# Hash attention and an MLP on one core: when squares, loads and block transposes of the next batch are issued

## Chip, cores and metric

One core of a Trainium2 chip runs the whole program in one launch. The metric is the device time of an execution in microseconds (us); lower is better.

## What is computed

The reference takes q, k and v of 4 batches, 8 heads, 768 tokens and 64 columns, and a projection of 64 by 6. Each query and key gets a bucket number from the signs of its 6 projections; a query attends only to keys of its own bucket. The attention output, rearranged to 768 rows of 512 per batch, goes through a normalisation and a two-layer MLP with a residual:

```
q_bits = (q @ proj > 0);  q_bucket = sum(q_bits * 2**arange(6))      # k likewise
scores = where(q_bucket == k_bucket, q @ k.T / 8, -1e9)
attn   = softmax(scores);  x = (attn @ v) as (4, 768, 512)
xn     = (x - mean(x)) / sqrt(var(x) + 1e-6) * g_ln
out    = x + relu(xn @ w_ch1) @ w_ch2                                  # 512 -> 2048 -> 512
```

## The kernel before

**Chunks.** The work is cut into 12 chunks, three of 256 queries for each batch, numbered 0 to 11; chunk n belongs to batch n // 3. A chunk's attention (`att_units`, L397) is 12 groups: for each, four score matmuls (L417), one exponential on ScalarE (L423) and eight value matmuls (L451). The scores of a group are emitted before the values of the group ahead of it. The MLP of a chunk (`mlp_steps`, L484) runs one chunk later: `norm` on VectorE (L523), a DMA transpose of the normalised rows into `xnT` (L541, on SP's queue), eight `up` steps (L568) that read `xnT`, and eight `down` steps (L590), the latter still one chunk later.

**The stage "chunk n"** (n = 3 to 11) therefore holds on TensorE: the 12 groups of chunk n, first the `down` steps of chunk n - 2 and then the `up` steps of chunk n - 1. `interleave` (L652) emits them: after the scores of the next group come the "lone" operations of this group (`lone[u]`, L676), then fillers up to a share of the chunk. `norm` is the first filler. The string of `plan` (L778) for chunk n has three parts: the first two are mixed with the two halves of the `down` steps, the last with the `up` steps.

**Preparing a batch** (class `Prep`, L184) takes, for each half of four heads:
- `L`, `load_half` (L136): q and k from memory into `qnat` and `knat`, natural layout. For batches 2 and 3 these are two DMAs of 384 KB for each of q and k, on SP's queue. Each of the two tile names has four buffers, so a load of batch b waits until the same half of batch b - 2 is done with.
- `W`, `load_values` (L159): one DMA of 768 KB into `vnat`, which has one buffer; `V` (L340) casts it on GpSimd and adds sums.
- `N`, `narrow` (L242): a cast on GpSimd to `nat16`; `T`, `operands` (L269): a DMA transpose of `nat16` into `slots` (L272), and behind it a DMA that copies the odd tokens within `slots` (L279).
- `B`, `blocks` (L250): four 32x32 block transposes on VectorE; `H`, `hashes` (L281): 32 hash matmuls, two VectorE operations, a DMA of the bits to a buffer in memory (L301, `bits_d`), and four DMAs that bring the bit rows back into `slots` (L303); these wait until `bits_d` has landed.
- `Q`, `squares` (L198): four ScalarE activations for each half that square q and k in place and accumulate the sums, for a check at the end. They are the last reader of `qnat` and `knat`.
- `E`, `share` (L353): one matmul and a copy.

**What sets the order.** Chunks 0, 1 and half of 2 are written out by hand (`first_two`, L696, table `also`). From there on the scheduler of the language may move instructions on each engine and queue, save those that are marked `tc.keep_in_program_order`. Before, the squares, the block transposes and the DMA transposes of batches 2 and 3 are marked, the loads are not. Each engine and SP's queue run their instructions strictly in order: a DMA that has to wait holds every DMA behind it on SP.

`alone` (L794) and `spread` (L798) put the block transposes and squares at groups: `B`s at the first four groups of the chunk, `Q`s evenly over the rest.

Of the kernel before, what the change touches and what calls it, by code (L numbers as in the profile page):

```python
# [28 lines left out]
def kernel(  # L29
# [11 lines left out]
    nc = tc.nc  # L41
# [94 lines left out]
    def load_half(b, half):  # L136

        h0 = half * H // 2
        t = {}
        for nm in "qk":  # L140
            t[nm] = nat.tile([P, H // 2, NC, D], F32, tag=f"{nm}nat", name=f"{nm}nat")

        if b == 0 and half == 0:
            nc.scalar.dma_start(out=proj1[0:D, 0, 0:n_bits], in_=proj)
        cuts = [[0, 1, 2, 4] if half == 0 else [0, 2, 4], [0, 4], [0, 2, 4], [0, 2, 4]][b]
        for lo, hi in zip(cuts, cuts[1:]):
            for nm, src in (("q", q), ("k", k)):
                eng = nc.gpsimd if b == 1 else nc.scalar if nm == "k" and hi - lo == 1 else nc.sync
                eng.dma_start(
                    out=t[nm][:, lo:hi],  # L150
                    in_=src[b, h0 + lo : h0 + hi].rearrange("h (p c) d -> p h c d", p=P),
                )
        if b == 0 and half == 0:
            nc.scalar.activation(wake2[:, 0:1], wake2[:, 1:2], AF.Exp)
            t["v"] = load_values(b, half, 0, 2)
            load_values(b, half, 2, 4, t["v"])
        return t

    def load_values(b, half, lo=0, hi=None, t=None):  # L159
        hi = H // 2 if hi is None else hi  # L160
        h0 = half * H // 2
        eng = nc.gpsimd if (b, half) == (1, 0) else nc.sync
        if t is not None:
            pass
# [7 lines left out]
        eng.dma_start(  # L172
            out=t[:, lo:hi],
            in_=v[b, h0 + lo : h0 + hi].rearrange("h (p c) d -> p h c d", p=P),
        )
        return t

    def copy_by(eng, dst, src):
# [5 lines left out]
    class Prep:  # L184
# [13 lines left out]
        def squares(self, half, a, j):  # L198

            src = self.tiles[half]["qk"[a]][:, 2 * j : 2 * j + 2].rearrange("p h c d -> p (h c d)")  # L200
            col = (2 * self.b + half) * 2 + j
            tc.keep_in_program_order(
                nc.scalar.activation(src, src, AF.Square, accum_out=sq[:, a, col : col + 1])  # L203
            )

        def tokens(self, h, par):

# [61 lines left out]
        def operands(self, half):  # L269


            done = nc.sync.dma_start_transpose(  # L272
                out=self.pair_places(half)[:, :, 0, :],
                in_=self.nat16[half].rearrange("p h a c d -> p (h a c d)"),
            )
            if self.b > 1:
                tc.keep_in_program_order(done)
            dst = self.pair_places(half)
            nc.sync.dma_start(out=dst[0:D, :, 1, :], in_=dst[D:P, :, 0, :])  # L279

# [90 lines left out]
        def part(self, kind, half):  # L371

            if kind == "T":
                return [(0, lambda: self.operands(half))]
            if kind == "H":
                return [(1300, lambda: self.hashes(half))]
            if kind == "N":
# [318 lines left out]
    def first_two():  # L696
# [8 lines left out]
        def keep_awake(n, pool=ps_mm, tag="mm"):  # L705
# [50 lines left out]
            16: [lambda: nxt.operands(0)],  # L756
# [19 lines left out]
            units[n][u][1]()  # L776

    plan = {  # L778
# [6 lines left out]
    }  # L785

    def prepare(text):
# [10 lines left out]
    def spread(text, n):  # L798

        ops = [f for _, f in prepare(text)]  # L800
        first = len(ops) if n < 2 * NP else 4 * text.count("B")
        rest = n - first
        out = [[f] for f in ops[:first]] + [[] for _ in range(rest)]
        for i, f in enumerate(ops[first:]):
            out[first + i * rest // (len(ops) - first)].append(f)
        return out

    def mixed(a, b):

# [9 lines left out]
    for n in range(2, len(chunks)):  # L819
# [19 lines left out]
        interleave(units[n][FIRST if n == 2 else 0 :], fillers, after, begun=True, lone=spread(alone.get(n, ""), 3 * NP - (FIRST if n == 2 else 0)))  # L839
# [190 lines left out]
```

## Time and profile before

| What | Value |
|---|---|
| Median of 3 runs | 323.79 us (323.53 to 324.67) |
| The profiled execution, own time | 321.0 us |
| Its span, first to last instruction | 319.2 us |
| Granted TensorE clock, mean | 0.995 |
| TensorE matmuls busy | 304.4 us, 95% |
| ScalarE / VectorE / GpSimd busy | 215.9 / 182.6 / 79.8 us |
| Chain that ended last | TensorE 82%, VectorE 7%, DMA 5% |

Times in the traces below count from the start of the span, in us. A row of the timeline has the start, the duration, the engine (SPq is SP's queue of DMA issues, PE is TensorE), the line, the operation, "output<-input" and a count; brackets hold the time that the engine sat idle just before, and what ended that idle time. For a DMA the duration is that of the issue, not of the transfer. A row of the windows view has the stretch, its length, the busy time of each engine with a count, the granted clock, the busy share of the DMA engines and what they moved.

### The profile page before, as it was taken

What the parts mean: (1) busy time and instruction counts of PE and PEld (TensorE: products, weight loads), DVE (VectorE), ACT (ScalarE), POOL (GpSimd) and SP (SyncE); (2) the same over time, 40 slices, a digit from 0 to 9 for tenths busy, and PEclk for the clock granted to TensorE, in tenths of its full rate; (3) what the DMA queues carried; (4) which work ended last, traced back from release to release, by engine and by line L of the source; (5) the groups of instructions that cost most, each with busy time, mean ns of one, the idle gap of its engine ahead of it and who ended that gap; (6) DMA issues with size and microseconds to landing.
All of it is one profiled execution on the core that took longest, in us unless ns stands there. A gap on an engine that the chain in (4) does not pass through costs nothing.

```text
span 319.2 us, 7982 instructions
## 1 busy us (share of the span) xinstructions
PE 304.4 (95%) x3338; PEld 227.1 (71%) x3338; DVE 182.6 (57%) x410; ACT 215.9 (68%) x273; POOL 79.8 (25%) x101
## 2 busy tenths in 40 slices
PE   7899989999999989999999999999999999999992
PEld 6565677858768748769768778778679688686661
DVE  1779965854674775646774774543634634446321
ACT  3688785855658857977768868979767568673110
POOL 3745210096060281044171160200200200202000
PEclk9999999999999999999999999999999999999998
DMA  7999999359696397492583183030110410200201
GB/s 242 362 216 316 196 316 107 69 133 236 157 241 145 97 289 167 138 271 101 197 167 97 11 164 98 11 93 9 35 66 2 43 58 2 68 35 14 87 11 66
DMA packets 65035, 40.95 MB, mean 128 GB/s; under 512 B 47216, under 2 KB 60016, under 8 KB 64992
## 3 DMA queue, kind: packets, MB, share of 16 engines
q1 hardware_dynamic: 60528, 31.85, 41.4%
q0 software_dynamic: 4096, 8.13, 10.9%
q8 instruction: 28, 0.46, 0.6%
q10 hardware_dynamic: 368, 0.39, 0.4%
q14 instruction: 15, 0.12, 0.1%
HBM read 27.98 MB, written 6.88 MB: 109 GB/s over the span
## 4 chain that ended last, share of the span: by engine, by line
PE 82%; DVE 7%; DMA 5%; ACT 2%; issue 2%; ACTq 0%; DVEq 0%
PE hp L568 25%; PE o L590 24%; PE sc L417 17%; PE av L451 9%; DVE slots L182 4%; DMA xnT<-xn 4%; PE hash L288 3%; ACT ex L423 2%; DMA knat<-in_k_dram 1%; DVE bits L324 1%; PE tpose L223 1%; PE hash L319 1%; DVE x L476 1%; ACT qnat L203 1%; DVE qkT L233 0%
## 5 line engine op out<-in xcount | busy, mean ns | idle before, releaser
L423 ACT ACTIVATE ex<-sc,expb 128x1024 bf16<-128x1024 f32 x144 | 159.9, 1116 | 64.5 <-PE sc L417 64.2
L568 PE MATMUL hp<-xnT,w_sb 128*128 128x256 bf16 x768 | 97.9, 273 | 2.5 <-DMA xnT<-xn 2.1
L590 PE MATMUL o<-w_sb,hbuf 128*128 128x512 bf16 (+1 forms) x400 | 95.7, 370 | 0.0
L417 PE MATMUL sc<-slots 70*128 70x256 bf16 x576 | 87.8, 272 | 1.8 <-DVE slots L182 1.7
L568 PEld LDWEIGHTS <-w_sb 128*128 128x128 bf16 x768 | 72.7, 98 | 12.4 <-DMA xnT<-xn 2.7
L451 PEld LDWEIGHTS <-ex 128*128 128x128 bf16 x1152 | 53.7, 98 | 18.1 <-ACT ex L423 3.1
L417 PEld LDWEIGHTS <-slots 70*128 70x128 bf16 x576 | 50.6, 97 | 16.3 <-issue 2.7
L451 PE MATMUL av<-vaug,ex 128*128 128x65 bf16 x1152 | 59.3, 194 | 0.9 <-ACT ex L423 0.8
L129 DVE TENSOR_SCALAR hbuf<-hp 128x512 bf16<-128x512 f32 x47 | 32.5, 691 | 46.8 <-PE hp L568 45.9
L590 PEld LDWEIGHTS <-hbuf 128*128 128x128 bf16 x400 | 36.9, 97 | 27.1
L546 POOL TENSOR_SCALAR rs<-mv 128x2 f32<-128x2 f32 x11 | 7.0, 635 | 153.8 <-DVE mv L531 153.7
L133 ACT ACTIVATE hbuf<-hp 128x512 bf16<-128x512 f32 x49 | 29.2, 596 | 18.5 <-PE hp L568 18.4
L595 DVE SCALAR_TENSOR_TENSOR x<-o,rs,x 128x512 f32<-128x512 f32 (+1 forms) x25 | 18.0, 719 | 32.3 <-PE o L590 32.3
L476 DVE TENSOR_TENSOR x<-x,rc 128x256 f32<-128x256 f32 x36 | 19.2, 533 | 1.0
L468 DVE TENSOR_SCALAR rc<-av 128x4 f32<-128x4 f32 x36 | 5.7, 157 | 21.8 <-PE av L451 21.8
L248 POOL CAST nat<-qnat 128x1536 bf16<-128x1536 f32 x6 | 8.9, 1489 | 29.9 <-DMA qnat<-in_q_dram 27.7
L532 DVE SCALAR_TENSOR_TENSOR xn<-x,mv,gbc 128x512 bf16<-128x512 f32 x22 | 15.5, 741 | 0.1
L469 DVE TENSOR_TENSOR x<-av,vsum 128x256 f32<-128x256 f32 x36 | 14.9, 415 | 0.0
L530 DVE BATCH_NORM_STATS2 stats<-x 128x6 f32<-128x512 f32 x22 | 14.0, 675 | 0.1
L203 ACT ACTIVATE knat<-knat 128x768 f32<-128x768 f32 x16 | 13.5, 841 | 0.0
L203 ACT ACTIVATE qnat<-qnat 128x768 f32<-128x768 f32 x16 | 13.4, 838 | 0.0
L253 DVE STREAM_TRANSPOSE bt<-qnat 128x768 f32<-128x768 f32 x12 | 11.6, 970 | 2.7 <-DMA qnat<-in_q_dram 2.6
(88 smaller groups left out, 213.9 us busy)
## 6 DMA issues: line engine op xcount, KB each, us to landing
out_dram<-x SPq DMA_DIRECT2D x23, 256.0 KB
vnat<-in_v_dram SPq DMA_DIRECT2D x6, 768.0 KB
qnat<-in_q_dram SPq DMA_DIRECT2D x11, 384.0 KB
knat<-in_k_dram SPq DMA_DIRECT2D x11, 384.0 KB
w_sb<-in_moe_w_ch_dram POOLq DMA_DIRECT2D x4, 1024.0 KB, 16.0
slots<-slots SPq DMA_DIRECT2D x6, 384.0 KB
qnat<-in_q_dram POOLq DMA_DIRECT2D x2, 768.0 KB, 20.8
knat<-in_k_dram POOLq DMA_DIRECT2D x2, 768.0 KB, 22.1
```

Of the source, the lines that this page charges most:

```text
L129: nc.vector.tensor_scalar_max(dst, src, 0.0)
L133: nc.scalar.activation(dst, src, AF.Relu if relu else AF.Copy)
L203: nc.scalar.activation(src, src, AF.Square, accum_out=sq[:, a, col : col + 1])
L417: nc.tensor.matmul(sc[:, i, :], sl[0:K1, h, 1, kj * P : (kj + 1) * P], sl[0:K1, h, 0, q0 : q0 + CT],)
L423: nc.scalar.activation(ex, sc, AF.Exp, bias=expb[:, 1:2] if b else expb[:, 0:1], scale=scale if b else scale / Q_SCALE,)
L451: nc.tensor.matmul(av[:, h - ha, qi, :], state[g][:, i, qi * P : (qi + 1) * P], va[:, h, CMAP[b][kj], :], start=(b > 0 and (g, i, qi) == ( ...
L469: nc.vector.tensor_tensor(xv, num, vs[:, ha : ha + 2, :].unsqueeze(2).to_broadcast([P, 2, TT, D]), op=AOP.add,)
L476: nc.vector.tensor_tensor(xv, num, rc.unsqueeze(3).to_broadcast([P, 2, TT, D]), op=AOP.mult)
L532: nc.vector.scalar_tensor_tensor(xn[:, :, i, :], x[:, i, :].rearrange("p (o d) -> p o d", d=P), mv[:, i, 0:1], gbc.rearrange("p (o d) -> p ...
L568: nc.tensor.matmul(hp[:, i, :], w1_sb[:, dt, nt * P : (nt + 1) * P], st["xnT"][:, dt, :], start=(dt == 0), stop=(dt == ND - 1),)
L590: nc.tensor.matmul(o2, st["h"][:, nt, i * P : (i + 1) * P], w2_sb[:, nt, cols], start=(nt == 0), stop=(nt == NH - 1),)
L595: nc.vector.scalar_tensor_tensor(x[:, i, cols], o2, st["rs"][:, i : i + 1], x[:, i, cols], op0=AOP.mult, op1=AOP.add,)
```

## The change

- **Squares.** The squares of batch 0, half 0 move from chunk 2 to four groups at the end of `first_two`; those of every later half move one chunk ahead (batch 0, half 1 from chunk 3 to chunk 2, and so on; chunk 8 keeps four of its eight). No chunk has more than four.
- **Loads.** The loads of batches 2 and 3 (q, k and v) are marked to stay in program order on SP, and `plan` puts most of them into its middle part: behind the DMA transpose of the same chunk and ahead of the hashes.
- **Odd tokens.** The copy of odd tokens becomes a step of its own, `O`, with its own place in the plan.
- **Blocks of batch 2, half 0** move from groups 0 to 3 of chunk 3 to groups 2 to 5.

In the built program the DMAs of SP's queue stand in this order around chunks 2 to 5 (the names are those of the plan; "bits" is L301, "rows" the four of L303):

```
before  T11 W20 out O11 bits L20a rows L20b out xnT(3) | out T20 O20 L21(q q) out bits rows x2 L21(k k) rows x2 W21 xnT(4)
        | out T21 O21 L30(q q) out bits rows x2 L30(k k) rows x2 W30 xnT(5)
after   T11 L20(q) out L20(k q k) O11 bits out W20 rows x4 xnT(3) | out T20 O20 L21(q k q k) out bits rows x4 xnT(4)
        | out T21 O21 W21 L30(q k q k) out bits rows x4 xnT(5)
```

```
 def load_half(b, half):
...
-                eng.dma_start(
+                done = eng.dma_start(
...
+                if b > 1:
+                    tc.keep_in_program_order(done)
...
 def load_values(b, half, lo=0, hi=None, t=None):        # likewise
...
 def squares(self, half, a, j):
-            tc.keep_in_program_order(
-                nc.scalar.activation(src, src, AF.Square, accum_out=sq[:, a, col : col + 1])
-            )
+            done = nc.scalar.activation(src, src, AF.Square, accum_out=sq[:, a, col : col + 1])
+            if (self.b, half) > (0, 0):
+                tc.keep_in_program_order(done)
...
+        def odd_tokens(self, half):                    # was the end of operands
+
             dst = self.pair_places(half)
             nc.sync.dma_start(out=dst[0:D, :, 1, :], in_=dst[D:P, :, 0, :])
...
-            24: [ups[2]],
-            25: [ups[3], lambda: nxt.hashes(0)],
-            26: [ups[4], lambda: nxt.blocks(1, 0, 0)],
-            27: [ups[5], lambda: nxt.blocks(1, 0, 1)],
+            24: [ups[2], lambda: prep.squares(0, 0, 0)],
+            25: [ups[3], lambda: nxt.hashes(0), lambda: prep.squares(0, 0, 1)],
+            26: [ups[4], lambda: nxt.blocks(1, 0, 0), lambda: prep.squares(0, 1, 0)],
+            27: [ups[5], lambda: nxt.blocks(1, 0, 1), lambda: prep.squares(0, 1, 1)],
...
     plan = {
-        2: "V10 N11 W11 | T11 H11 L20 | E10 V11 W20",
-        3: "E11 N20 | T20 L21 | H20",
-        4: "V20 W21 L30 N21 | T21 | H21 E20",
-        5: "V21 W30 L31 | E21",
-        6: "V30 W31 N30 | T30 | H30 E30",
-        7: "V31 N31 | T31 | H31 E31",
+        2: "V10 N11 W11 | T11 L20 O11 H11 | E10 V11 W20",
+        3: "E11 N20 | T20 O20 L21 | H20",
+        4: "V20 N21 | T21 O21 W21 L30 | H21 E20",
+        5: "V21 | W30 L31 | E21",
+        6: "V30 N30 | T30 O30 W31 | H30 E30",
+        7: "V31 N31 | T31 O31 | H31 E31",
     }
...
     alone = {
-        2: "Q00", 3: "B20 Q01", 4: "B21 Q10", 5: "Q11", 6: "B30 Q20", 7: "B31 Q21", 8: "Q30 Q31",
+        2: "Q01 QQQQ..",
+        3: "B20 Q10 ..BBBBQ.Q.QQ",
+        4: "B21 Q11 BBBBQ.Q.Q.Q.",
+        5: "Q20 Q..Q..Q..Q..",
+        6: "B30 Q21 BBBBQ.Q.Q.Q.",
+        7: "B31 Q30 BBBBQ.Q.Q.Q.",
+        8: "Q31 Q..Q..Q..Q..",
     }
```

`spread` now reads these strings: one character for each group, a dot for none.

More of the change, by code (lines that the diff above doesn't have):

```diff
@@ L171, in load_values @@
             t = nat.tile([P, H // 2, NC, D], F32, tag="vnat", bufs=1, name="vnat")
-        eng.dma_start(
+        done = eng.dma_start(
             out=t[:, lo:hi],
@@ L175, in load_values @@
         )
+        if b > 1:
+            tc.keep_in_program_order(done)
         return t
@@ L201, in squares @@
             col = (2 * self.b + half) * 2 + j
-            tc.keep_in_program_order(
-                nc.scalar.activation(src, src, AF.Square, accum_out=sq[:, a, col : col + 1])
-            )
+            done = nc.scalar.activation(src, src, AF.Square, accum_out=sq[:, a, col : col + 1])
+            if (self.b, half) > (0, 0):
+                tc.keep_in_program_order(done)
         def tokens(self, h, par):
@@ L374, in part @@
                 return [(0, lambda: self.operands(half))]
+            if kind == "O":
+                return [(0, lambda: self.odd_tokens(half))]
             if kind == "H":
@@ L794, with spread @@
     alone = {
-        2: "Q00", 3: "B20 Q01", 4: "B21 Q10", 5: "Q11", 6: "B30 Q20", 7: "B31 Q21", 8: "Q30 Q31",
-    }
[L798 to L806, printed above, removed]
+        2: "Q01 QQQQ..",
[5 more added lines that the diff above has]
+        8: "Q31 Q..Q..Q..Q..",
+    }
+    def spread(text):
+        *ops, places = text.split()
+        todo = {op[0]: [f for _, f in prepare(op)] for op in ops}
+        return [[todo[c].pop(0)] if c != "." else [] for c in places]
     def mixed(a, b):
@@ L838 @@
             after = units[n + 1][0]
-        interleave(units[n][FIRST if n == 2 else 0 :], fillers, after, begun=True, lone=spread(alone.get(n, ""), 3 * NP - (FIRST if n == 2 else 0)))
+        interleave(units[n][FIRST if n == 2 else 0 :], fillers, after, begun=True, lone=spread(alone[n]) if n in alone else ())
     tc.no_sync_barrier()
```

2 lines of the change are left out of this document (1 added, 1 removed).

## The prediction

> **What bounds the kernel now.** I read the page's chain of work first, then the busy times by chunk, then the idle time of TensorE, and last SP's queue, because the idle time led there.
>
> ```profile
> PE 82%; DVE 7%; DMA 5%; ACT 2%; issue 2%; ACTq 0%; DVEq 0%
> ```
>
> TensorE sets the end; no other engine is worth shortening for itself. The windows view shows where TensorE's time is more than its work. The stretches run from the first `down` matmul of one chunk to that of the next: the end of the hand-written part, then chunks 3, 4, 6, 8 and 10. The last two rows are stretches in which the loads fill the DMA engines.
>
> ```profile
> 46.80:61.80 15.00, 14.72 (x196) 12.48 (x194) 9.35 (x17) 10.63 (x13) 0.00 (x0) 1.00 0.78 109
> 82.35:106.98 24.63, 24.03 (x275) 18.08 (x273) 14.55 (x33) 18.09 (x25) 5.51 (x5) 1.00 0.78 176
> 106.98:132.60 25.62, 24.09 (x275) 18.02 (x273) 17.01 (x36) 17.96 (x25) 10.03 (x11) 1.00 0.67 178
> 154.88:178.80 23.92, 23.92 (x276) 18.10 (x274) 15.66 (x36) 17.91 (x25) 8.82 (x9) 1.00 0.58 140
> 202.70:225.10 22.40, 22.34 (x242) 16.99 (x240) 10.67 (x29) 20.61 (x33) 1.72 (x2) 1.00 0.13 37
> 247.50:269.80 22.30, 22.30 (x243) 17.03 (x241) 10.80 (x32) 15.03 (x17) 1.71 (x2) 1.00 0.22 37
> 111.20:117.40 6.20, 6.20 (x56) 3.64 (x54) 6.17 (x12) 4.16 (x5) 4.87 (x6) 1.00 0.92 265
> 143.00:145.00 2.00, 2.00 (x32) 1.78 (x30) 1.73 (x5) 0.69 (x2) 1.45 (x2) 1.00 1.06 392
> ```
>
> Chunks 3, 4 and 6 hold the same TensorE work (275 or 276 matmuls). Chunk 6 takes 23.92 us, chunk 3 24.63 (0.71 more), chunk 4 25.62 (1.70 more). Chunk 8, with eight squares on ScalarE (20.61 us busy), takes 22.40 against 22.30 in chunk 10, which has none: 0.10. So 0.71 + 1.70 + 0.10 = 2.51 us is all that an order of squares and loads can win behind the hand-written part. The timeline of TensorE says what was late:
>
> ```profile
> 93.58 1.05 PE L568 MATMUL hp<-xnT,w_sb 128*128 128x256 bf16 x8 [0.60 <-DMA xnT<-xn]
> ...
> 119.04 1.05 PE L568 MATMUL hp<-xnT,w_sb 128*128 128x256 bf16 x8 [1.53 <-DMA xnT<-xn]
> ```
>
> The first `up` step of chunks 3 and 4 waits for the transposed rows `xnT`, 0.60 and 1.53 us; some 0.15 each is lost in starting again (0.71 - 0.60, 1.70 - 1.53). So `xnT` was needed at 93.58 - 0.60 = 92.98 and at 119.04 - 1.53 = 117.51.
>
> **Why it was late.** The timeline of SP's queue, which issues DMAs in order; first the bit rows ahead of chunk 3's `xnT`, then an `xnT` issue of chunk 7 by itself, then chunks 3 to 6:
>
> ```profile
> 82.45 3.05 SPq L303 DMA_DIRECT2D slots<-bits_d  x4
> ```
>
> ```profile
> 183.26 1.28 SPq L541 DMA_TRANSPOSE xnT<-xn  x1
> ```
>
> ```profile
> 91.88 4.14 SPq L272 DMA_TRANSPOSE slots<-nat  x1
> 97.74 0.68 SPq L279 DMA_DIRECT2D slots<-slots  x1
> ...
> 108.10 1.53 SPq L303 DMA_DIRECT2D slots<-bits_d  x2
> 110.09 0.92 SPq L149 DMA_DIRECT2D knat<-in_k_dram  x2
> 111.07 1.49 SPq L303 DMA_DIRECT2D slots<-bits_d  x2
> 112.67 0.79 SPq L172 DMA_DIRECT2D vnat<-in_v_dram  x1
> 113.57 1.77 SPq L541 DMA_TRANSPOSE xnT<-xn  x1
> 115.44 0.53 SPq L599 DMA_DIRECT2D out_dram<-x  x1
> 116.25 4.60 SPq L272 DMA_TRANSPOSE slots<-nat  x1
> 122.53 0.68 SPq L279 DMA_DIRECT2D slots<-slots  x1
> ...
> 131.90 1.54 SPq L303 DMA_DIRECT2D slots<-bits_d  x2
> ...
> 162.12 3.77 SPq L272 DMA_TRANSPOSE slots<-nat  x1
> 167.72 0.67 SPq L279 DMA_DIRECT2D slots<-slots  x1
> ...
> 175.01 3.05 SPq L303 DMA_DIRECT2D slots<-bits_d  x4
> ```
>
> In chunk 4 the two k loads and the v load, 2 x 384 + 768 KB, are issued just ahead of `xnT`, which lands 119.04 - 113.57 = 5.47 us after its issue. With no load ahead, a transpose of three times the size (162.12) lets its successor go at 167.72, 1.83 us after its own 3.77 of issue; so an unhindered `xnT` needs about 1.28 + 1.83 = 3.1 us (an estimate). The queue moves data in the order of issue.
>
> The second thing in these rows is the wait of the bit rows for `bits_d` to land, since `bits_d` too lies behind the loads. From the copy of the odd tokens to the rows it is 175.01 - 167.72 = 7.29 us with no load between, 131.90 - 122.53 = 9.37 and 108.10 - 97.74 = 10.36 with one pair of q loads (768 KB) between.
>
> **The change, part by part.** The price of 768 KB of load ahead of something on the queue is the quantity on which all hangs; call it r.
>
> ```profile
> qnat<-in_q_dram SPq DMA_DIRECT2D x11, 384.0 KB
> ```
>
> A pair of q or k loads is 2 x 384 KB, as much as one v load. These 786,432 bytes at the 265 GB/s of the stretch from 111.20 are 2.97 us; at the 392 GB/s of the one from 143.00, 2.0. The waits give 9.37 - 7.29 = 2.1 to 10.36 - 7.29 = 3.1. If the wait grew in proportion to everything between (384 KB of odd tokens and 768 of q make 10.36 us), 768 KB would be 6.9: no row is near that. I take **3.0**, because the 265 GB/s row and the 10.36 wait both lie there; 2.0 and 3.6 stay for the range.
>
> *Chunk 3, a gain.* The loads of batch 2, half 0 (1536 KB) now stand ahead of `bits_d` where the v load (768) stood, and v follows behind it. Rows: 82.45 + 3.0 = 85.45; their four issues take 3.05; `xnT` at 88.5, lands at 91.6. The v load behind `bits_d` has drained by then (85 + 3.0). Needed 92.98: no wait, **-0.71**. VectorE has the normalised rows earlier, since the blocks left groups 0 and 1.
>
> *Chunk 4, a smaller gain.* The transpose of batch 2, half 0 stays at 91.88 (it follows an output that waits for TensorE), its copy goes 5.60 later, at 97.5 instead of 97.74. All four q and k loads now stand ahead of `bits_d`, one pair more: rows at 108.10 - 0.25 + 3.0 = 110.85, done at 113.9. That is where `xnT` was issued before, but nothing lies ahead of it: it lands at 117.0. Needed 117.51 - 0.71 = 116.8, a wait of 0.2 and 0.15 for the restart: of 1.70 us, 1.35 is won, **-1.35**.
>
> *Chunk 5, a new wait.* Before, its `up` steps began without one:
>
> ```profile
> 143.32 1.04 PE L568 MATMUL hp<-xnT,w_sb 128*128 128x256 bf16 x8
> ```
>
> Now the transpose of half 1 goes at 113.9 + 1.28 + 0.53 = 115.8, its copy of odd tokens 5.60 later at 121.4. Behind it come v **and** four q and k loads, 2304 KB where 768 were: two more prices. Rows at 121.4 + 9.37 + 2 x 3.0 = 136.8, issued by 139.8, then `xnT`, landing at 142.9. TensorE, by now 0.71 + 1.35 us earlier, and another 0.1 because a `share` matmul moves behind the first `up` steps, wants it at 143.32 - 2.16 = 141.15. A wait of 1.75 and the restart: **+1.9**. Behind `xnT` on SP stand only outputs and loads for chunk 6 and later; TensorE has nothing else to do, as all eight `down` steps come first.
>
> *Chunk 6.* The v load now lies ahead of its bits, but from the rows' end at 178.06 to `xnT` at 183.26 there are 5.2 us, more than r: nothing. *Chunk 8* loses four squares: **-0.1**.
>
> *The squares in the hand-written part.* Four more squares on ScalarE, each with a read of its sum, at the four groups from about 50 us on:
>
> ```profile
> L203 ACT ACTIVATE qnat<-qnat x16: 832/833/867, 63.1 to 218.2; 128x768 f32<-128x768 f32 x16
> L203 ACT ACTIVATION_READ_ACCUMULATOR qnat<-qnat x16: 189/192/224, 63.8 to 218.9; 128x1 f32 x16
> ```
>
> 4 x (0.83 + 0.19) = 4.1 us on top of 10.63 in 15.00: it fits, but the last two lie close.
>
> ```profile
> 57.28 1.11 ACT L423 ACTIVATE ex<-sc,expb 128x1024 bf16<-128x1024 f32 x1 [0.44 <-PE sc L417]
> 58.29 0.59 ACT L133 ACTIVATE hbuf<-hp 128x512 bf16<-128x512 f32 x1
> 58.95 1.11 ACT L423 ACTIVATE ex<-sc,expb 128x1024 bf16<-128x1024 f32 x1
> ```
>
> ```profile
> 61.13 0.41 PE L451 MATMUL av<-vaug,ex 128*128 128x65 bf16 x8
> ```
>
> The third square uses up the 0.44 of idle and pushes the rest by 0.6, the fourth by 1.0 more: the exponential of 58.95 would end at 58.95 + 1.6 + 1.11 = 61.7, 0.5 after its values at 61.13. Consecutive starts are 0.1 closer than the durations, which takes it down to 0.1 or 0.2: **+0.15**, from 0 to 0.5. Without this cover (TensorE waiting for all of it) it would be 4.1. The squares of the later chunks keep their number and spacing; the block transposes stay early enough for the hashes. No cost.
>
> **Sum:** -0.71 - 1.35 + 1.9 - 0.1 + 0.15 = -0.1. The profiled execution's 321.0 would stay at 320.9; the median of the runs shown is 2.8 above that execution, so 323.79 becomes **323.7**. What is won at chunks 3 and 4 is given back at chunk 5.
>
> **The rivals.**
>
> *The loads are quick, all 2.5 us are won.* With r = 2.0, chunk 4 waits no more (-1.70), its rows end at 112.9; chunk 5's copy is at 120.4, its rows at 120.4 + 9.37 + 4.0 = 133.8, `xnT` lands at 139.9, needed at 140.8: no wait. -0.71 - 1.70 - 0.1 + 0.15 = -2.4: **321.4**. It decides from r = 2.5 downwards. For it: the 392 GB/s row, and the wait of 9.37. Against: the longer row at 265. The same comes out if the rows do not wait as I think. The Trainium skill, page "DMA: Bandwidth & Descriptors", section "Anatomy of one DMA — SWDGE (gpsimd) path", fits the variable part of a DMA issued from GpSimd as bytes over 436 GB/s; by that 768 KB would be 1.8 us (an estimate from the page) and this rival would be right; the stretch from 111.20 shows 265 GB/s, and the quickest row 392.
>
> *Slower: the queue in chunk 5 is worse than I think.* One mechanism: 2304 KB ahead of `bits_d`. The rows of chunk 5 move by three times what r moves, once through chunk 4's `xnT` and twice by their own loads. At r = 3.7: chunk 4 wins 0.65, `xnT` of chunk 5 lands at 145.0 against 141.85 needed, +3.3; sum +2.0: **325.8**. It counts as slower from r = 3.55. For it: 10.36 us of wait with one pair. Against: no stretch of loads as slow as 786 KB / 3.55 us = 220 GB/s.
>
> *ScalarE:* the exponentials stay late over several groups and TensorE pays one square, 1.0 us: **324.6**.
>
> *The change doesn't do what it says:* the built order of SP's queue has the loads where the plan puts them, so I give this nothing.
>
> **How the numbers follow.** Forecast (r from 2.5 to 3.55) 0.58, own range 322.2 to 325.3; all won 0.22; slower 0.14; ScalarE 0.06. A measurement here tells about 0.5% (1.6 us) from no change. Faster by more: 0.22. Slower by more: 0.15 (the slower case and a little of ScalarE's). Within: 0.63. The range takes in the 321.4 of the first rival and reaches up to 325.5.
>
> **What would show it.** Right: SP's rows (L303) start near 85.4, 110.9 and 136.8; no idle before the first `up` of chunk 3, at most some tenths at chunk 4, and a new idle of about 1.7 us with releaser `xnT` in chunk 5. Chunk 8 at 22.3. Wrong if chunk 5 has no idle (the first rival), if the idle at chunk 4 stays above 1, or if the values near 61 wait for ScalarE by more than 0.5.

## The result, and the profile after

| | before | after |
|---|---|---|
| Median of the runs | 324.23 us (323.53 to 325.32, 4 runs) | 320.20 us (319.17 to 321.47, 4 runs) |
| The profiled execution, own time / span | 321.0 / 319.2 us | 321.47 / 319.7 us |
| Mean granted clock of the profiled execution | 0.995 | 0.998 |

The changed kernel takes 0.9875 of the time before (95% interval 0.9825 to 0.9924). A second measurement gave 0.9855 (0.9792 to 0.9919); the ratios leave out runs that lie more than 1.5% above the fastest of their kernel. The forecast was no change, 323.7 us, with a range that took in 321.4 and reached up to 325.5: the kernel is faster, and lies below 321.4.

The table holds something odd at once: the two *profiled* executions take the same time, while the medians lie 4.0 us apart. So the stages have to be compared one by one. The chain that ended last holds less of VectorE and DMA than before, whose line had 7% and 5%:

```profile
PE 87%; DVE 5%; DMA 2%; issue 2%; ACT 1%; ACTq 0%; DVEq 0%
```

The windows view of after, in the same stretches as before (end of the hand-written part, then chunks 3, 4, 5 and 8; the columns are those of the view of before):

```profile
48.15:64.31 16.16, 14.72 (x196) 12.46 (x194) 9.36 (x17) 13.12 (x20) 0.00 (x0) 1.00 0.67 79
84.86:108.72 23.86, 23.86 (x276) 18.16 (x273) 15.29 (x33) 17.26 (x23) 4.54 (x4) 1.00 0.82 187
108.72:132.64 23.92, 23.92 (x276) 18.11 (x274) 15.48 (x36) 18.78 (x27) 8.86 (x10) 1.00 0.65 159
132.64:155.58 22.94, 22.59 (x244) 17.15 (x241) 11.66 (x30) 18.30 (x26) 8.92 (x11) 1.00 0.64 196
203.41:225.58 22.17, 22.17 (x243) 17.02 (x241) 10.69 (x29) 18.31 (x26) 1.72 (x2) 1.00 0.13 37
```

In chunks 3 and 4 TensorE's busy time equals the length of the stretch: the waits of 0.60 and 1.53 us are gone. Chunk 5 lacks 0.35. Lengths of the stretches in us, from the first `down` matmul of one chunk to that of the next, for two executions of each kernel (the second ones are the profiles of the first two experiments below):

| stretch | before | before, again | after | after, again |
|---|---|---|---|---|
| start to the first `up` | 46.79 | 48.74 | 48.14 | 48.03 |
| rest of the hand-written part | 15.02 | 14.23 | 16.17 | 15.12 |
| chunk 3 | 24.63 | 24.76 | 23.86 | 25.14 |
| chunk 4 | 25.62 | 27.91 | 23.92 | 23.92 |
| chunk 5 | 22.28 | 22.27 | 22.94 | 22.41 |
| chunk 8 | 22.41 | 22.40 | 22.17 | 22.17 |
| chunks 3 + 4 + 5 + 8 | 94.94 | 97.34 | 92.89 | 93.64 |

From chunk 6 on the other stretches agree within 0.1 us. So after is 2.05 us better in its four chunks than the first profile of before, and 4.45 better than the second. The first profile of after gave 2.5 us back ahead of chunk 2 (48.14 + 16.17 against 46.79 + 15.02). Of that, 1.44 us is an idle time within the hash matmuls, put down to issue:

```profile
56.83 0.52 PE L295 MATMUL hash<-bt,proj 128*32 128x192 f32 x3 [1.44 <-issue]
```

The second execution of after has 0.39 us of it, and before has 0.28 and none. The start up to the first `up` varies from 46.6 to 53.1 us over the 14 profiles of this study. With the change's start e10 reaches chunk 2 at 61.70, as early as before. So the 2.5 us are no fixed cost of the change; whether the moved squares make the idle time within the hash matmuls more frequent isn't shown (the two above 1 us, here and in e8, are both in kernels that have them).

SP's queue in after: rows of chunk 3, then chunk 4 and chunk 5, each from the copy of odd tokens (L286) over the loads (L149 q and k, L174 v) and `bits_d` (L308) to the rows (L310) and `xnT` (L550).

```profile
87.53 3.05 SPq L310 DMA_DIRECT2D slots<-bits_d  x4
90.69 1.28 SPq L550 DMA_TRANSPOSE xnT<-xn  x1
...
99.58 0.67 SPq L286 DMA_DIRECT2D slots<-slots  x1
100.34 0.91 SPq L149 DMA_DIRECT2D qnat<-in_q_dram  x1
...
104.66 0.56 SPq L308 DMA_DIRECT2D bits_d<-bits  x1
111.69 3.46 SPq L310 DMA_DIRECT2D slots<-bits_d  x4
115.27 1.29 SPq L550 DMA_TRANSPOSE xnT<-xn  x1
...
124.08 0.68 SPq L286 DMA_DIRECT2D slots<-slots  x1
124.81 0.90 SPq L174 DMA_DIRECT2D vnat<-in_v_dram  x1
...
137.18 3.03 SPq L310 DMA_DIRECT2D slots<-bits_d  x4
140.32 1.29 SPq L550 DMA_TRANSPOSE xnT<-xn  x1
```

From odd tokens to rows it is 12.11 us with two pairs of loads between (111.69 - 99.58), and 13.10 with two pairs and v (137.18 - 124.08). The forecast for the latter was 9.37 + 2 x 3.0 = 15.4. TensorE's timeline shows what chunk 5 waits for in the end:

```profile
143.75 1.05 PE L577 MATMUL hp<-xnT,w_sb 128*128 128x256 bf16 x8 [0.35 <-DMA xnT<-xn]
```

0.35 us, where the prediction had 1.75. The marks that the prediction named for the rows were 85.4, 110.9 and 136.8; they stand at 87.53, 111.69 and 137.18. Taking off the 2.5 us that this execution had lost ahead of chunk 2, that is 85.0, 109.2 and 134.7: right for chunk 3 within 0.4, and then earlier by 1.7 and 2.1.

### The profile page after: what moved, and what is told of

Its sections match the earlier page's. It is cut to its first block, busy times and chain, and to the rows that moved or that the text cites. A ratio compares the mean times of both kernels' runs of the same rounds, so it can differ in the third digit from the quotient of the medians.

```text
span 319.7 us, 7980 instructions
## 1 busy us (share of the span) xinstructions
PE 303.7 (95%) x3338; PEld 227.2 (71%) x3338; DVE 181.3 (57%) x410; ACT 215.7 (67%) x273; POOL 79.6 (25%) x101
## 4 chain that ended last, share of the span: by engine, by line
PE 87%; DVE 5%; DMA 2%; issue 2%; ACT 1%; ACTq 0%; DVEq 0%
PE hp L577 26%; PE o L599 25%; PE sc L426 18%; PE av L460 10%; DVE slots L186 3%; PE hash L295 3%; DMA knat<-in_k_dram 1%; PE hash L326 1%; ACT ex L432 1%; DMA xnT<-xn 1%; PE tpose L227 1%; DVE bits L331 1%; DVE hbuf L129 0%; PE av L451 0%; DVE qkT L237 0%
## 5 line engine op out<-in xcount | busy, mean ns | idle before, releaser
L349 POOL CAST vaug<-vnat 128x1536 bf16<-128x1536 f32 x6 | 8.8, 1472 | 34.8 <-DMA vnat<-in_v_dram 34.8
L485 DVE TENSOR_TENSOR x<-x,rc 128x256 f32<-128x256 f32 x36 | 16.9, 470 | 1.0
```

The lines of the kernel that those rows point to most:

```text
L485: nc.vector.tensor_tensor(xv, num, rc.unsqueeze(3).to_broadcast([P, 2, TT, D]), op=AOP.mult)
```

## The experiments

Three explanations are weighed. **Cheap loads**: the price r of 768 KB ahead of `bits_d` is well under 3.0 us, so that chunk 5 loses nothing; that is the prediction's first rival. **One part alone**: the squares or the loads by themselves bring the gain. And, formed after the first four runs and called C where an expectation uses letters, **the clock**: a long wait of TensorE costs more than itself, because the clock is halved behind it.

| run | what it is | median, us (runs) | ratio to before (95% interval) |
|---|---|---|---|
| e1_before_again | before | 323.45 (12) | 0.9979 (0.9931 to 1.0028) |
| e2_after_again | after | 320.10 (6) | 0.9855 (0.9792 to 0.9919) |
| e3_squares_only | squares alone | 323.75 (12) | 0.9961 (0.9908 to 1.0014) |
| e4_loads_only | loads alone | 323.04 (12) | 0.9991 (0.9949 to 1.0033) |
| e5_loads_behind_bits | after, loads behind the bits | 324.33 (12) | 1.0007 (0.9970 to 1.0043) |
| e6_wake_in_before | before, waits filled with matmuls | 322.91 (12) | 0.9966 (0.9928 to 1.0004) |
| e7_late_xnt | after, one `xnT` late | 321.37 (12) | 0.9955 (0.9921 to 0.9990) |
| e8_late_xnt_awake | the same, wait filled | 321.90 (12) | 0.9961 (0.9932 to 0.9989) |
| e9_later_xnt | after, one `xnT` later still | 323.28 (12) | 0.9976 (0.9936 to 1.0016) |
| e10_later_xnt_awake | the same, wait filled | 322.42 (12) | 0.9974 (0.9933 to 1.0014) |
| e11_blocks_early | after, blocks back at groups 0 to 3 | 319.79 (4) | 0.9878 (0.9800 to 0.9957) |
| e12_v_behind | after, v loads behind the bits | 324.09 (12) | 0.9973 (0.9926 to 1.0020) |

e1 to e4, e5 to e8 and e9 to e12 each ran in one session on one chip, with runs of before beside them: 323.81, 323.48 and 324.15 us (29, 35 and 29 runs).

### Both kernels again

No edit.

> The kernel before, unchanged, timed against itself, with a second profile. Theory Q (queue): what the change wins is the wait of TensorE for xnT in chunks 3 and 4, given back in part in chunk 5; in the two profiles that is 24.63 + 25.62 + 22.28 us before against 23.86 + 23.92 + 22.94 after, 1.8 us, and 0.2 in chunk 8, 2.0 in all, while the 1.4 to 2.5 us by which the changed kernel's profile was later up to 64 us is chance of that one execution. Then this kernel's profile shows the same chunk lengths again (24.6, 25.6, 22.3) and its time up to the first up step can differ by 1 us or more from 46.8. Theory S (start): the hand-written part itself differs for good between the two kernels; then this profile has its first up step at 46.8 and its last hand-written group at 61.8 again, within 0.3. Ratio 1.000, and its interval tells how small an effect these rounds can see.

> The changed kernel, timed again with a second profile. The first comparison gave 0.9875, that is 4.0 us, where the chunk lengths of the two profiles explain 2.0. Theory Q: the ratio comes nearer to 1 - 2.0/324 = 0.994, and the profile has chunks 3, 4, 5 at 23.9, 23.9, 22.9 (a wait of about 0.5 for xnT in chunk 5). Theory S: the ratio stays at 0.9875 and the difference shows up to 64 us, where the squares were added (earlier than in the kernel before, not later).

The ratio of after did not come nearer to 0.994, as the queue theory expected: it is 0.9855. The start of before took 48.74 us this time, so it isn't fixed to the kernel, as the start theory has it. And the chunks of before did not repeat: the second profile has the same two waits, and the longer one is longer. The row of chunk 4's first `up` step, and the windows around it:

```profile
120.98 1.23 PE L568 MATMUL hp<-xnT,w_sb 128*128 128x256 bf16 x8 [2.18 <-DMA xnT<-xn]
```

```profile
108.28:121.72 13.44, 11.15 (x99) 6.88 (x99) 9.38 (x19) 7.97 (x10) 7.33 (x9) 1.00 0.72 178
121.72:125.13 3.41, 3.41 (x26) 2.57 (x24) 1.66 (x5) 1.53 (x2) 2.70 (x3) 0.50 1.00 183
125.13:136.19 11.06, 11.06 (x154) 9.55 (x153) 4.43 (x12) 8.47 (x14) 0.00 (x0) 1.00 0.51 142
```

The column behind the five engines is the granted clock. 0.74 us after the wait had ended it fell to 0.50 for 3.41 us, while TensorE was fully busy; half of 3.41, 1.7 us of work, is lost. The chunk's 27.91 us are 3.99 more than chunk 6's 23.92: a wait of 2.18, the clock 1.70, and 0.1 of restart. In the profile on which the prediction rests, the wait was 1.53 us and the clock stayed at 1.00.

After, again, has no wait in chunk 4 and none to speak of in chunk 5 (22.41). It has one in chunk 3, since that execution's rows of chunk 3 were issued only at 88.88, because `bits_d` had landed late. 120 of its 128 packets had ended by 85.21, the other 8 ended from 87.71 to 88.19.

```profile
95.44 1.05 PE L577 MATMUL hp<-xnT,w_sb 128*128 128x256 bf16 x8 [1.11 <-DMA xnT<-xn]
```

So chunk 3's gain isn't always had; chunk 4's is, in both. Five kernels below (e7 to e11) keep after's order in these chunks, and their profiles agree: chunk 4 takes 23.91 or 23.92 us in all seven, chunk 3 23.86 or 23.87 in six, chunk 5 22.41 or 22.42 in five (22.94 in the first of after, 23.13 in e10).

### Squares alone

Before, with the new strings of squares, the blocks at groups 0 to 3 and the loads left to the scheduler:

```
+            24: [ups[2], lambda: prep.squares(0, 0, 0)],
...
+        2: "Q01 QQQQ..",
+        3: "B20 Q10 BBBBQ.Q.Q.Q.",
...
     # plan and load_half as before
```

> The kernel before with the squares moved as in the change (four at the end of the hand-written part, each later half one chunk ahead, four per chunk) and nothing else: loads not marked, old plan, blocks of batch 2 at groups 0 to 3. The scheduler now puts v and four q or k loads between the bit rows and xnT of chunk 3, and q, k and v between the rows and xnT of chunk 4. Theory Q: xnT still lies behind loads, so the waits stay or grow: 0.6 or more in chunk 3, 1.5 or more in chunk 4; time within 0.3% of the kernel before or slower by up to 2 us. Rival (the squares are what wins, since ScalarE is freed and buffers come free earlier): 2 us or more faster, waits in chunks 3 and 4 gone.

The squares free their buffers a chunk sooner, and the scheduler uses that at once: it moves all four q and k loads, with the v load, between chunk 3's rows and its `xnT`. SP's queue, then TensorE:

```profile
82.14 3.05 SPq L303 DMA_DIRECT2D slots<-bits_d  x4
85.24 0.50 SPq L172 DMA_DIRECT2D vnat<-in_v_dram  x1
85.85 0.44 SPq L149 DMA_DIRECT2D qnat<-in_q_dram  x1
...
87.36 0.61 SPq L149 DMA_DIRECT2D knat<-in_k_dram  x1
88.08 2.05 SPq L541 DMA_TRANSPOSE xnT<-xn  x1
```

```profile
96.78 1.05 PE L568 MATMUL hp<-xnT,w_sb 128*128 128x256 bf16 x8 [2.50 <-DMA xnT<-xn]
```

`xnT` is issued at 88.08 and used at 96.78, 8.70 us later, against 3.43 in after's chunk 5 (143.75 - 140.32). The wait of 2.50 again has 3.41 us at a clock of 0.50 behind it (from 97.75), and chunk 3 takes 28.14, 4.28 more than after's. The expectation had the wait of chunk 4 stay as well; it went: that chunk, now free of loads, takes 23.92. The gain is there and is lost a chunk earlier: what the squares do is to let loads move; where the loads go decides.

### Loads alone

After, with the squares in the chunks where they were:

```
-            24: [ups[2], lambda: prep.squares(0, 0, 0)],
+            24: [ups[2]],
...
-        4: "B21 Q11 BBBBQ.Q.Q.Q.",
+        4: "B21 Q10 BBBBQ.Q.Q.Q.",
...
-        8: "Q31 Q..Q..Q..Q..",
+        8: "Q30 R31 QQ.QQ.RR.RR.",
```

> The changed kernel with the squares where they were (none in the hand-written part, one chunk later, eight in chunk 8); loads in program order and the new plan stay. Loads now wait on SP for the squares of their buffer, with bit rows and xnT behind them. Theory Q: three of four loads of chunk 3 are issued only as the squares end (about 98 to 107 us), one row DMA after them; xnT of chunk 4 still goes out at about 112 with no load behind which it queues much: the wait in chunk 4 is under 0.5 and 1.5 to 2.5 us are won, about as with the whole change, since its order is what counts. Rival (squares ahead are needed, or the loads stall SP): SP waits for the squares hold xnT up, the wait in chunk 4 or 5 is 1.5 us or more and the kernel is no faster than before.

Chunks 3 and 4 win as in after (23.86 and 23.92), but the rival of the expectation came true in chunk 5: it takes 26.33. With the squares a chunk later, the buffers of the loads come free later, and in the built order three of the four loads stand behind the first row:

```profile
133.56 0.78 SPq L310 DMA_DIRECT2D slots<-bits_d  x1
134.45 0.44 SPq L149 DMA_DIRECT2D knat<-in_k_dram  x1
134.94 0.58 SPq L149 DMA_DIRECT2D qnat<-in_q_dram  x1
135.56 0.46 SPq L149 DMA_DIRECT2D knat<-in_k_dram  x1
136.07 2.24 SPq L310 DMA_DIRECT2D slots<-bits_d  x3
138.41 2.36 SPq L550 DMA_TRANSPOSE xnT<-xn  x1
```

```profile
143.72 1.18 PE L577 MATMUL hp<-xnT,w_sb 128*128 128x256 bf16 x8 [2.11 <-DMA xnT<-xn]
```

The wait of 2.11 and a clock of 0.50 from 144.49 to 147.90 make up 3.82 of the 3.92 us by which it exceeds 22.41. Neither half of the change brings the gain alone.

### Loads behind the bits

If it is the loads ahead of `bits_d` that cost, they can go behind the rows:

```
-        3: "E11 N20 | T20 O20 L21 | H20",
-        4: "V20 N21 | T21 O21 W21 L30 | H21 E20",
+        3: "E11 N20 | T20 O20 | H20 L21",
+        4: "V20 N21 | T21 O21 | H21 E20 W21 L30",
```

> The changed kernel with the loads of chunks 3 and 4 (batch 2 half 1; then v and batch 3 half 0) moved behind the hashes in the plan, so that bits_d and the four rows go first on SP. Theory Q (bits_d lies behind the loads on the queue and holds xnT up): the rows of chunk 5's stage start about 7 us after the odd tokens instead of 13, xnT of chunk 5 goes out when VectorE has the rows (about 135 in place of 140) and chunk 5 takes 22.3 to 22.4 instead of 22.4 to 22.9; chunk 3 is as in the changed kernel (23.9 to 25.1); time 0.3 to 0.7 us below the changed kernel. Rival (the loads now lie ahead of xnT itself and cost the same): chunks 4 or 5 wait 0.5 us or more, no gain over the changed kernel or a loss.

With the loads behind, the wait from odd tokens to rows falls to 7.57 and 7.02 us (99.92 to 107.49, 128.29 to 135.31), as the expectation had it; before's chunk 6, without loads, has 7.29. But it isn't faster, as the rival had it: chunk 4 takes 28.91. VectorE's timeline says why:

```profile
109.14 0.42 DVE L485 TENSOR_TENSOR x<-x,rc 128x256 f32<-128x256 f32 x1
114.12 0.98 DVE L257 STREAM_TRANSPOSE bt<-qnat 128x768 f32<-128x768 f32 x1 [4.55 <-DMA qnat<-in_q_dram]
115.02 1.25 DVE L539 BATCH_NORM_STATS2 stats<-x 128x6 f32<-128x512 f32 x2
```

A block transpose of the next half waits 4.55 us for the late q load, and the `norm` of chunk 4 stands behind it on VectorE; `xnT` is issued at 119.01 only, and TensorE waits 2.93. In chunk 5, too, `xnT` goes out behind five loads, at 141.55, and TensorE waits 1.20 (23.79 us). That is the other bound of the place for the loads: late enough for `xnT`, and ahead of the blocks.

### Keeping TensorE busy in the waits

The clock can be tried by filling a wait with matmuls of zeros. First in before, whose waits are as they come (the added matmuls go into a buffer that the `up` step overwrites):

```
     def up(n2):
...
+        if n2 == 0:
+            for _ in range({(0, 2): 12, (1, 0): 24}.get((b, t), 0)):
+                nc.tensor.matmul(hp[:, 0, 0:P], wake, wake)
```

> The kernel before with 12 extra matmuls of zeros ahead of the first up step of chunk 3 and 24 ahead of that of chunk 4, into the tile that this step overwrites. xnT comes as late as before; only TensorE's idle time is filled. In the profiles so far a wait for xnT of 2.1 to 2.5 us was followed 3 us later by 3.4 us at half the granted clock (kernel before again, squares only, loads only), a wait of 1.5 or less was not. Theory C (clock): much of what the change wins beyond the 1.8 us of waits is this half clock; then here its runs have a mean granted clock of 0.993 or more (15 of 41 runs of the kernel before lie below 0.9925) and the median falls by 0.5 to 1.5 us. Rival (the clock falls by itself, or the waits alone count): as many runs below 0.9925 as before, and the time the same or up to 1 us longer for the added matmuls.

```profile
83.83:109.56 25.73, 24.69 (x288) 18.82 (x286) 15.73 (x33) 18.21 (x25) 5.62 (x6) 1.00 0.76 170
109.56:134.84 25.28, 25.28 (x300) 19.48 (x298) 16.34 (x36) 17.97 (x25) 9.53 (x11) 1.00 0.74 181
```

The profile shows chunk 4 without idle time and with a clock of 1.00 (chunk 3 keeps 1.04 us of idle). One such period in mid-run takes about 0.005 off an execution's mean clock (1.7 of 320 us). In the 14 profiles the mean tells the two kinds apart: eight have no half clock ahead of their last matmul and means of 0.993 to 0.998, six have one or two such periods and means of 0.985 to 0.992. Here 4 of 12 executions had a mean below 0.9925, against 8 of 35 of before beside it, as the rival had it; the median is 0.57 us lower (322.91 against 323.48), as theory C had it. The runs decide nothing.

So the next kernels make the wait themselves, in a chunk that has none. In after, seven (e7) or nine (e9) DMAs of the normalised rows into a buffer that nobody reads stand ahead of the `xnT` that is read in chunk 10; e8 and e10 add 36 and 48 matmuls of zeros ahead of its first `up` step:

```
+                if (b, t) == (B - 1, 0):
+                    for i in range(7):               # e9: 9
+                        tc.keep_in_program_order(
+                            nc.sync.dma_start(out=dump[i], in_=xn.rearrange("p o i d -> p (o i d)"))
+                        )
...
+            if n2 == 0 and (b, t) == (B - 1, 0):     # e8: 36, e10: 48
+                for _ in range(36):
+                    nc.tensor.matmul(hp[:, 0, 0:P], wake, wake)
```

> The changed kernel with seven DMAs of 256 KB (the normalised rows to a buffer in memory that nobody reads) on SP between the normalised rows and xnT of chunk 10, where nothing else loads the queue: xnT is made late on purpose. Each takes about 0.9 us, so xnT lands some 6 us later, 2 to 3 us after TensorE wants it. Theory C: chunk 10 grows from 22.3 by the wait plus up to 1.7 us of half clock, the mean granted clock falls to about 0.990 in most runs, and the kernel is 3 to 5 us slower than the changed one. Rival: it grows by the wait alone, clock unchanged.

> As the kernel with the late xnT, with 36 matmuls of zeros (about 2 us) ahead of the up step that waits for it. Theory C: same landing of xnT, but no half clock: mean clock at 0.993 or more in most runs, and 1 to 1.7 us faster than without the matmuls of zeros. Rival (the clock does not follow TensorE's idle time): no difference in clock or time between the two.

e7's wait came out at 1.46 us:

```profile
259.28 1.05 PE L585 MATMUL hp<-xnT,w_sb 128*128 128x256 bf16 x8 [1.46 <-DMA xnT<-xn]
```

Chunk 10 takes 23.79 against 22.16 (after, again), 1.63 more: the wait and 0.17. There was no half clock, so the pair couldn't tell the theories apart; e8's matmuls cost more than the wait they cover (24.17). The wait had to be longer.

> As the changed kernel with the late xnT of chunk 10, with nine DMAs of 256 KB ahead of it instead of seven. Seven made TensorE wait 1.5 us and the clock did not fall. At about 0.75 us each, nine make it wait about 3.0 us, longer than the 2.1 to 2.9 after which 3.4 us at half clock were seen. Theory C: the profile has 3.4 us at 0.5 behind that wait, chunk 10 takes 22.2 + 3.0 + 1.7 = 27 us, most runs have a mean clock below 0.9925, and the kernel is 4 to 5 us slower than the changed one. Rival (waits alone): chunk 10 takes 25.3, clock as in the changed kernel.

> The same nine DMAs, and 48 matmuls of zeros (about 2.7 us) ahead of the up step that waits. Theory C: no fall of the clock behind the wait, chunk 10 takes about 25.4 and the runs are 1.5 us or more faster than without the matmuls of zeros, with few mean clocks below 0.9925. Rival: the same time and clock as without them.

e9, the row and the windows:

```profile
264.02 1.03 PE L585 MATMUL hp<-xnT,w_sb 128*128 128x256 bf16 x8 [2.10 <-DMA xnT<-xn]
```

```profile
262.00:265.33 3.33, 1.31 (x15) 1.19 (x15) 0.97 (x4) 1.01 (x1) 0.00 (x0) 1.00 0.91 228
265.33:268.74 3.41, 3.41 (x18) 2.44 (x17) 0.53 (x1) 1.71 (x2) 0.00 (x0) 0.50 0.00 0
```

e10, where the matmuls of zeros lie in the wait, and its whole chunk 10:

```profile
256.27 2.84 PE L584 MATMUL hp<-wake 128*128 128x128 bf16 x48
```

```profile
245.67:270.70 25.03, 25.00 (x290) 19.73 (x289) 10.79 (x30) 14.93 (x16) 1.71 (x2) 1.00 0.39 127
```

0.6 us more of wait than in e7 made chunk 10 2.28 us longer (26.07 against 23.79), and the difference is the half clock. With the same late `xnT` and TensorE busy, 25.03. Of e9's executions 9 of 11 had a mean clock below 0.9925 (a twelfth, of 1103 us, is left out), of e10's 3 of 12. The medians, 323.28 and 322.42, lie the right way round, with intervals that overlap. Where in an execution the clock fell can be seen only in the profiled one; of the others the mean alone is known. That matmuls of zeros count as work for the clock is seen in e11's start: 26 of them from 0.98 us on are all that TensorE does up to 3.73, and the clock rises at 3.77.

### Where the blocks and the v load stand

```
e11:
-        3: "B20 Q10 ..BBBBQ.Q.QQ",
+        3: "B20 Q10 BBBBQ.Q.Q.Q.",
e12:
-        4: "V20 N21 | T21 O21 W21 L30 | H21 E20",
-        5: "V21 | W30 L31 | E21",
+        4: "V20 N21 | T21 O21 L30 | H21 E20",
+        5: "W21 | V21 L31 | E21 W30",
```

> The changed kernel with one part undone: the block transposes of batch 2, half 0 back at groups 0 to 3 of chunk 3. Its loads reach the buffers at 84 to 88 us in the changed kernel, the chunk begins at 84. Theory Q: the blocks wait for the loads on VectorE with norm behind them, so xn is 1 to 3 us later, xnT of chunk 3 goes out at 92 or later either way; chunk 3 takes 0 to 2 us more than 23.9 to 25.1. Rival (the place of the blocks is of no account): chunk 3 unchanged.

> The changed kernel with the v load of batch 2, half 1 moved from ahead of chunk 5's bits to behind chunk 5's xnT, and the next v load behind it. Theory Q with 1.8 us for 768 KB: the rows of chunk 5's stage start 11.2 us after the odd tokens instead of 13.1, xnT goes out 1.9 us earlier and lands in time: chunk 5 takes 22.3 instead of 22.4 to 22.9; time 0.1 to 0.6 us below the changed kernel, which these rounds can hardly tell. Rival (768 KB cost 3.0 us as predicted, or v was not what held the bits): the rows start 10 us after, or still 13.

e11 is as fast as after (319.79 against 320.20 and 320.10), and its chunks 3, 4 and 5 hold no wait at all (23.86, 23.92, 22.41): the rival is right, and where these blocks stand plays no part. e12 takes 768 KB from ahead of chunk 5's `bits_d`. The rows then start 12.24 us after the odd tokens (121.58 to 133.82), where after's order has 12.63 to 13.42: 0.4 to 1.2 us earlier, not the 1.9 of the expectation. And it loses more than it could win:

```profile
149.10 0.37 PE L363 MATMUL share<-vs,epsk 128*128 128x256 bf16 x1 [4.47 <-POOL vs L358]
```

```profile
143.95 1.47 POOL L349 CAST vaug<-vnat 128x1536 bf16<-128x1536 f32 x1 [8.72 <-DMA vnat<-in_v_dram]
...
148.40 0.65 POOL L358 TENSOR_TENSOR vs<-vsum,vaug 128x256 bf16<-128x256 f32 x1
```

The v load arrives late, GpSimd's cast and sums with it, and the `share` matmul waits 4.47 us at the head of TensorE. Chunk 5 takes 28.32, with a half clock behind this wait too (148.70 to 152.12).

## Why the prediction was wrong

Point by point, in us, first profile of before against first of after:

| step | forecast | measured | verdict |
|---|---|---|---|
| chunk 3 | -0.71 | -0.77 (after, again: +0.51) | right, not in every execution |
| chunk 4 | -1.35 | -1.70 | right, a little more |
| chunk 5 | +1.9 | +0.66 (after, again: +0.13) | **wrong** |
| chunk 8 | -0.1 | -0.24 | right, a little more |
| squares in the hand-written part | +0.15 | no wait for ScalarE (the stretch itself +1.15) | right, as far as shown |
| sum | -0.1 | -2.05 for the four chunks | |

**What bounds the kernel** was read rightly: TensorE, and in chunks 3 and 4 the `xnT` behind loads. The waits that the prediction found are those that went. Chunk 8 won more than forecast because the prediction's stretch of chunk 10 begins at 247.50, ahead of its first `down` matmul at 247.62: chunk 10 takes 22.16, so chunk 8 stood 0.25 above it and not 0.10.

**The squares in the hand-written part.** They run (ScalarE 13.12 against 10.63 us busy), and no matmul of that stretch waits for ScalarE in after. With them the stretch took 14.23 to 16.17 us (14.23 in e3 and e9), without them 14.23 to 15.02 (14.23 in e1 and e6): they need not cost anything, and what is longer in the first profile of after is the 1.44 us of idle within the hash matmuls.

**Chunk 5 is the step that failed**: "2304 KB where 768 were: two more prices", each at "3.0, because the 265 GB/s row and the 10.36 wait both lie there". The mechanism was right, loads ahead of `bits_d` hold the rows and so `xnT`; its size was wrong. One pair more (chunk 4) made the wait 12.11 against 10.36 before, +1.75; two prices more (chunk 5) made it 13.10 against 9.37, +3.73 or 1.87 each; in after, again, 12.63, 1.63 each. All 14 profiles together, from the copy of odd tokens to the rows of chunks 4 to 6 (e4's chunks 4 and 5, with half a pair among them, are left out):

| 768 KB loads ahead of `bits_d` | wait, us (cases) | mean | step |
|---|---|---|---|
| none | 5.87 to 7.69 (8) | 7.0 | |
| one | 8.62 to 10.54 (16) | 9.7 | 2.7 |
| two | 11.21 to 12.44 (9) | 11.9 | 2.1 |
| three | 12.63 to 13.42 (7) | 13.1 | 1.2 |

The first load costs most here, and the change adds second and third ones, at 2.1 and 1.2. The range of 2.0 to 3.6 came from the rate of one stretch and from the wait of one execution, and the prediction took the end where two rows lay. The rate was no price: 265 GB/s was what moved in that stretch, not what could. Here the page "DMA: Bandwidth & Descriptors" of the Trainium skill (section "Anatomy of one DMA — SWDGE (gpsimd) path"), which the prediction quoted with bytes over 436 GB/s, was nearer with 1.8 us (an estimate from the page): the second and third load cost 1.7 on average. The page's fit is for DMAs issued from GpSimd, and these loads go out on SP's queue.

With r under 2.5 the prediction's own rival "the loads are quick, all 2.5 us are won" gives 321.4. Its mechanism is what happened, and 2.05 of its 2.4 us were had in the first profiles.

**The second failure is what no step contains: what a wait costs beyond itself.** 321.4 is still 1.2 above the 320.20. The sum was made against a profile 2.8 us under the median of its own kernel, and the prediction carried that 2.8 over as if the change couldn't touch it. The profiles of this study say what a wait of TensorE costs (extra length against the same chunk without a wait):

| wait | us of wait | chunk longer by | clock behind it |
|---|---|---|---|
| e2, chunk 3 | 1.11 | 1.28 | 1.00 |
| e7, chunk 10 | 1.46 | 1.63 | 1.00 |
| before, chunk 4 | 1.53 | 1.70 | 1.00 |
| e9, chunk 10 | 2.10 | 3.91 | 0.50 for 3.41 us |
| e4, chunk 5 | 2.11 | 3.92 | 0.50 for 3.41 us |
| e1, chunk 4 | 2.18 | 3.99 | 0.50 for 3.41 us |
| e3, chunk 3 | 2.50 | 4.28 | 0.50 for 3.41 us |
| e5, chunk 4 | 2.93 | 4.99 | 0.50 for 3.41 us |
| e12, chunk 5 | 4.47 | 5.91 | 0.50 for 3.41 us, from 0.40 us before the wait ended |

Up to 1.53 us a wait costs itself and 0.17; from 2.10 on it costs 1.4 to 2.1 more than itself. Before's `xnT` in chunk 4 lies on either side of that from one execution to the next (1.53 and 2.18 in its two profiles).

The kept traces show more closely when the clock falls. In each of the 14 profiles every change of the granted clock lies on a grid with a step of 3.413 us: in e9 it rises at 12.74, falls at 36.63, rises at 40.05, falls at 265.33 and rises at 268.74, which is 7, 8, 74 and 75 steps after the first. From full speed it fell behind every window of this grid in which TensorE idled for 2.08 us or more, and, with one exception, behind none with 1.76 or less. A window of e7 without a fall, and the exception, the start of e4 with 1.34 us of idle:

```profile
256.03:259.44 3.41, 1.95 (x26) 1.29 (x23) 1.23 (x4) 1.45 (x2) 0.00 (x0) 1.00 1.09 259
259.44:262.85 3.41, 3.41 (x39) 3.07 (x38) 1.02 (x2) 1.99 (x3) 0.00 (x0) 1.00 0.15 55
```

```profile
35.26:38.68 3.42, 2.08 (x32) 1.37 (x27) 3.24 (x9) 2.30 (x3) 0.00 (x0) 1.00 1.24 205
38.68:42.09 3.41, 3.41 (x35) 2.91 (x35) 2.06 (x6) 1.96 (x2) 0.00 (x0) 0.50 1.18 255
```

So in these traces it is the idle time within one window that goes with the fall, and a wait that lies across an edge of the grid is split: before's 1.53 us at 118.01 into 0.5 and 1.0. The waits of 2.10, 2.11 and 2.18 in the table lay whole in one window.

The runs agree. Of the executions of the kernels whose profile has a wait of 2.10 us or more (e3, e4, e5, e9, e12) 44 of 59 had a mean clock below 0.9925; of e6, e7, e8 and e10 9 of 48; of before in the three sessions 37 of 104; of those with after's waits (after, e2, e11) 2 of 14. Executions of before with a low mean had a median of 326.4, 324.85 and 325.63 in the three sessions, the others 323.24, 323.32 and 323.53. Against the 323.24 of its session after's 320.10 is 3.1 better. Of that, 2.6 is the first profile of before against the four profiles of after's order that hold no wait in chunks 3 to 5 (e7, e8, e9, e11: 92.35 to 92.37 us for chunks 3, 4, 5 and 8); the rest, as far as the profiles let one argue, is the part of before's longer waits that is paid without a half clock. How the 4.0 us divide between waits and clock isn't measured.

The Trainium skill, page "TensorE: Matmul & The Clock Gate", section "Part 1: The HAM clock gate", has the clock fall to half after at least one idle window of about 3.4 us. The length of the period agrees here, 3.41 us. The idle time that it takes doesn't: 2.08 us of idle in a window of 3.41 were enough.

**Scalar and slower rivals.** ScalarE paid nothing. For the slower one r had to be 3.55; the loads that the change adds cost 2.1 and 1.2. What it named, a wait of some 3 us in chunk 5, is what e4 showed at 2.11, but from loads behind the rows and not ahead of them.

**What stays open.** How many of before's executions reach the half clock in chunk 4 and how many elsewhere isn't known, since only profiled ones show where. That filling the wait prevents it is borne out by the runs of e9 and e10 (9 of 11 and 3 of 12), not by those of e6; the profile of e10 alone doesn't show it, since its filled stretch lies across an edge of the grid (257.37). Why the clock fell in e4's start isn't known. No kernel here beats after; e11 equals it.

## What to carry to other kernels

A wait of the engine that sets the end has a price that jumps: read the granted clock behind it, and take a wait near 2 us as one that can cost 4. When the profiled execution lies away from the median of its own kernel, explain that gap first, since a change may act just there. And price a transfer on an in-order queue by how much later its successor gets, with one more and one less ahead of it, not by the rate of a stretch; the place of the loads has two bounds, the small transfer behind them and the first reader of what they bring.

## What the hardware showed that was not expected

- The half clock lasted 3.41 us each time (eight such periods ahead of the last matmul in these profiles, two of them in the start of e4 and e9), and its edges lay on the grid of 3.413 us that each trace has. Behind a wait it began 2.9 to 4.1 us after the wait had begun, mostly when TensorE already worked again.
- A DMA can land late by a few of its packets: 8 of the 128 of `bits_d` in chunk 3 of e2 ended 2.5 us or more behind the rest (0.6 us in the first profile of after), which put the rows at 88.88 and made a wait of 1.11 us.
- The start up to the first `up` step took 46.59 (e10) to 53.12 us (e9) in kernels that don't differ there. The clock is low at first: in e9 matmuls of zeros follow each other every 107 ns until 12.74 us and every 56 ns behind it. It rose at 3.77 to 12.74 us; the five executions in which it rose after 9 us took 48.74 to 53.12 us to the first `up`, the nine others 46.59 to 48.88. Much of the spread of the runs, 320.11 to 327.52 for before beside e1, can lie in it.
